# MoE1's second product with tokens on partitions, the domain weight applied where it leaves PSUM, and TensorE transposes to MoE2's input

## The chip, the cores and the metric

The kernel runs as one program on one core of a Trainium2 chip. The metric is device time in microseconds (us) of that core, from a launch with all inputs in HBM to the output in HBM. TensorE is called PE here, VectorE DVE, ScalarE ACT, GpSimd POOL and SyncE SP, as in the profile.

## The reference

Three steps follow one another on 2304 tokens (4 batches of 576) of 512 features.

```
# chunked attention: 8 heads of 64, chunks of 64 tokens
scores = (q_c @ k_c^T) / 8;  attn = softmax(scores);  x = attn @ v_c        # x: [2304, 512]
# MoE1: 4 experts, 512 -> 1024 -> 512
p = domain_probs / (domain_probs.sum(-1) + 1e-9)                            # [2304, 4], positive
x1 = sum over e of  p[:, e] * (max(x @ w1[e], 0) @ w2[e])
# MoE2: 512 -> 2048 -> 512
h = x1 @ w_in;  out = (h * clip(h + 3, 0, 6) / 6) @ w_out
```

All of it is fp32 to the caller, except that `w_in` and `w_out` arrive as 64-bit floats.

## The kernel before

**Blocks, sets, groups.** Tokens are cut into six blocks of 256 or 512 (`sizes`), and blocks are paired into three sets: 256 and 512, 512 and 256, 512 and 256. The hidden features of both MoEs are cut into groups of 512 columns: 8 groups for MoE1 (`G1`, two for each expert) and 4 for MoE2 (`G2`). In a set the order is group by group, and in a group first the one block, then the other. Only the first two groups of the first set run otherwise, in three parts of 256 tokens.

**Slots.** A group on a block is eight slots: four H slots (`h_slot`, first product, one per 128 hidden columns) and four Y slots (`y_slot`, second product). Each fp32 product is split: a tensor is kept as a high part that PE's fast fp32 format holds exactly and a low part, and three matmuls (high x high, high x low, low x high, the list `HL`) make one product. So an H slot is 12 matmuls of n columns, n the tokens of the block. In MoE1 a Y slot is also 12 matmuls of n columns: the weights are the stationary operand, the tokens move, and the result has features on partitions (four banks `psY`, one for each 128 features). In MoE2 the hidden activations are stationary, 512 weight columns move, and the result has tokens on partitions (n/128 banks), which is the layout of the output.

**What leaves PSUM.** PSUM has 2 banks for H, 4 for Y and 2 for attention. In MoE1 an H slot's bank is read by DVE alone (L434: u = max(psH, 0) * pb, where `pb` holds the domain weight of each token, broadcast over the partitions by a DMA from a scratch tensor in HBM). ACT then rounds u to the high part (L437), and one slot later DVE computes the low part u - high (L438). In MoE2 the bank is read by ACT (r = relu(psH + 3)) and one slot later by DVE (L447), followed by ACT's high part and DVE's low part (L451). After the fourth Y slot the Y banks are added into `acc` in SBUF (`finish`): by ACT's copy for the first group of a MoE, by DVE (L492) for the others. These additions are queued in `spread` and taken 2, 1, 1 and 0 at a time in the next four H slots. At MoE1's last group the sum is split again into MoE2's input x: high by ACT (L498), low by POOL (L499).

**What else runs.** Weights are loaded, rounded by ACT (L140) and subtracted by POOL (L141), 8 tiles for each group. In the first set's MoE1, from group 2 on, 32 tiles of MoE2's weights are turned from 64-bit to 32-bit floats (`Convert`): ACT takes absolute value and low word (L162, L163), DVE runs five operations (L167, L168, L171, L178, L182), POOL two (L183, L184). Two `cm` tiles limit how many are under way. Attention for the second and third set is computed in items of 512 columns, spread over the MoE slots of the set before.

**What sets the order.** All instructions are issued in an order that the program writes out. For each slot it issues: prepared loads (`pre`), the slot's matmuls, attention matmuls (`tail`), the low parts left from the slot before (`late`), attention's vector work (`early`), the slot's own reading of PSUM (`now`), some additions from `spread`, and the conversion steps (`post`). A planner, `fit`, puts attention and conversion steps into slots by an estimate of DVE's load in each slot (`busy`).

## Time and profile before

| | |
|---|---|
| time, median of 3 runs | 1328.59 us (1327.57 to 1329.6) |
| profiled execution | 1329.72 us, of which the span is 1327.9 us |
| PE busy | 1277.5 us (96%) |
| DVE busy | 696.8 us (52%) |
| ACT busy | 457.0 us (34%) |
| POOL busy | 504.3 us (38%) |
| mean granted clock of PE | 0.984 |

The span is the time from the first to the last instruction. The busy time of PE overlaps: matmuls are pipelined and their ends are modelled, so a busy PE is not a PE at its pace. Its pace is read from the distance between starts, which is what the chain of waits shows. "x <- y" names the tile written and the tiles read; L412 is line 412 of the kernel before. The shares above are averages over stretches with different limits, so the views below are taken by stretch.

### The profile page before, as it was taken

How to read it: one execution, taken by the hardware profiler on the slowest of the kernel's cores; microseconds unless marked ns; L12 is line 12 of the kernel's file. 1: busy time of each engine (PE TensorE's matmuls, PEld its weight loads, DVE VectorE, ACT ScalarE, POOL GpSimd, SP SyncE). 2: the span in 40 equal slices, each digit the busy share in tenths (PEclk: the TensorE clock that was granted, in tenths of full speed). 3: DMA queues.
4: the chain of work that ended last, by engine and by line, in shares of the span. 5: the costliest groups of instructions: out<-in, count | busy, mean ns of one | idle time of the engine just before them, and what ended most of it. 6: DMA issues, size and time to landing. Idle time of an engine off the chain costs nothing.

```text
span 1327.9 us, 20991 instructions
## 1 busy us (share of the span) xinstructions
PE 1277.5 (96%) x8134; PEld 1109.9 (84%) x8134; DVE 696.8 (52%) x1200; ACT 457.0 (34%) x914; POOL 504.3 (38%) x382
## 2 busy tenths in 40 slices
PE   8999889788999999999999999999999999999998
PEld 7998778676888888888888888888888888888887
DVE  5648999989555653233354544654233333333443
ACT  4343334333344432322222344343322222234432
POOL 3324766657542223333323262322333333344330
PEclk9999899889999999999999999999999999999999
DMA  7426555554333324222223233423222222222211
GB/s 191 127 75 188 174 172 166 170 146 136 92 91 105 87 72 123 70 69 69 71 81 94 62 89 103 112 65 104 83 72 68 72 68 72 68 64 64 64 32 48
DMA packets 172548, 128.86 MB, mean 97 GB/s; under 512 B 66720, under 2 KB 141984, under 8 KB 172448
## 3 DMA queue, kind: packets, MB, share of 16 engines
q1 hardware_dynamic: 172448, 127.52, 33.2%
q8 instruction: 64, 1.05, 0.3%
q14 instruction: 36, 0.29, 0.1%
HBM read 114.33 MB, written 13.14 MB: 96 GB/s over the span
## 4 chain that ended last, share of the span: by engine, by line
PE 80%; DVE 16%; ACT 2%; issue 1%; DMA 0%; SPq 0%; POOL 0%; ACTq 0%; DVEq 0%; POOLq 0%
PE psH L412 38%; PE psY L471 23%; PE psY L473 15%; DVE gt L438 3%; DVE cm L168 3%; DVE cm L171 2%; DVE cm L167 2%; DVE u L434 1%; DVE ce L178 1%; PE psS L306 1%; DVE acc L492 1%; DVE cm L182 1%; PE psP L338 1%; DVE e L330 1%; PE psX L349 1%
## 5 line engine op out<-in xcount | busy, mean ns | idle before, releaser
L412 PE MATMUL psH<-x,ws 128*128 128x256 f32 (+1 forms) x3552 | 634.9, 337 | 29.8 <-DVE u L434 27.5
L141 POOL TENSOR_TENSOR ws<-wr,ws 128x512 fp32r<-128x512 f32 x288 | 386.4, 1353 | 723.3 <-ACT ws L140 676.4
L412 PEld LDWEIGHTS psH<-x,ws 128*128 128x128 f32 x3552 | 550.5, 193 | 101.3 <-DVE u L434 31.1
L471 PE MATMUL psY<-gt,ws 128*128 128x256 f32 (+1 forms) x2400 | 413.2, 330 | 0.1
L471 PEld LDWEIGHTS psY<-gt,ws 128*128 128x128 f32 x2400 | 354.9, 188 | 49.4 <-DVE gt L438 0.5
L437 ACT CAST gt<-u 128x256 fp32r<-128x256 f32 (+1 forms) x200 | 100.1, 501 | 511.5 <-DVE u L434 510.8
L434 DVE SCALAR_TENSOR_TENSOR u<-psH,pb 128x256 f32<-128x256 f32 (+1 forms) x200 | 107.6, 538 | 313.4 <-PE psH L412 312.6
L473 PE MATMUL psY<-ws,gt 128*128 128x512 f32 x864 | 204.4, 393 | 0.0
L473 PEld LDWEIGHTS psY<-ws,gt 128*128 128x128 f32 x864 | 160.7, 188 | 34.3
L140 ACT CAST ws<-wr 128x512 fp32r<-128x512 f32 x288 | 171.1, 617 | 3.6 <-DMA wr<-in_moe_w_dram 2.9
L438 DVE TENSOR_TENSOR gt<-u,gt 128x256 fp32r<-128x256 f32 (+1 forms) x200 | 142.1, 711 | 56.2 <-ACT gt L437 54.5
L492 DVE TENSOR_TENSOR acc<-psY,acc 128x512 f32<-128x512 f32 (+1 forms) x226 | 125.4, 574 | 48.1 <-PE psY L473 36.1
L443 ACT ACTIVATE r<-psH,three 128x256 f32<-128x256 f32 (+1 forms) x96 | 55.7, 580 | 162.5 <-PE psH L412 161.2
L447 DVE SCALAR_TENSOR_TENSOR u<-r,psH 128x256 f32<-128x256 f32 (+1 forms) x96 | 53.0, 552 | 102.7 <-ACT r L443 101.9
L451 DVE SCALAR_TENSOR_TENSOR gt<-u,gt 128x256 fp32r<-128x256 f32 (+1 forms) x96 | 74.0, 771 | 41.5 <-ACT gt L450 41.4
L450 ACT ACTIVATE gt<-u 128x256 fp32r<-128x256 f32 (+1 forms) x96 | 50.6, 527 | 43.7 <-DVE u L447 43.5
L183 POOL TENSOR_TENSOR w<-w,ce 128x512 f32<-128x512 f32 x32 | 49.1, 1534 | 25.8 <-DVE ce L178 24.2
L184 POOL TENSOR_TENSOR ce<-w,cm 128x512 f32<-128x512 f32 x32 | 43.9, 1372 | 2.5
L499 POOL TENSOR_TENSOR x<-acc,x 128x256 fp32r<-128x256 f32 (+1 forms) x24 | 26.1, 1103 | 32.8 <-ACT x L498 32.8
L171 DVE SCALAR_TENSOR_TENSOR cm<-w,cm 128x512 uint32<-128x512 uint32 x32 | 35.8, 1118 | 1.1
L168 DVE TENSOR_SCALAR cm<-cm 128x512 uint32<-128x512 uint32 x32 | 33.4, 1045 | 1.1
L167 DVE TENSOR_SCALAR cm<-cm 128x512 f32<-128x512 f32 x32 | 29.3, 916 | 4.1 <-ACT cm L162 4.1
(45 smaller groups left out, 364.1 us busy)
## 6 DMA issues: line engine op xcount, KB each, us to landing
wr<-in_moe_w_dram SPq DMA_DIRECT2D x192, 256.0 KB, 2.8
wr<-win SPq DMA_DIRECT2D x48, 256.0 KB, 2.8
wr<-wout SPq DMA_DIRECT2D x48, 256.0 KB, 2.6
w<-in_moe_w_in_dram SPq DMA_DIRECT2D x16, 512.0 KB, 5.0
w<-in_moe_w_out_dram SPq DMA_DIRECT2D x16, 512.0 KB, 4.8
out_dram<-acc SPq DMA_DIRECT2D x18, 256.0 KB, 2.1
win<-ce SPq DMA_DIRECT2D x16, 256.0 KB, 3.5
wout<-ce SPq DMA_DIRECT2D x16, 256.0 KB, 3.0
```

The lines of the kernel that those rows point to most:

```text
L140: nc.scalar.copy(t[:, 0], self.t)
L141: (eng or nc.gpsimd).tensor_tensor(out=t[:, 1], in0=self.t, in1=raw(t[:, 0]), op=ALU.subtract)
L168: nc.vector.tensor_scalar(out=mu, in0=mu, scalar1=4, scalar2=1, op0=ALU.logical_shift_left, op1=ALU.logical_shift_right)
L171: nc.vector.scalar_tensor_tensor(out=mu, in0=self.t[:, :, 1], scalar=0x80000000, in1=mu, op0=ALU.bitwise_and, op1=ALU.bitwise_or)
L412: nc.tensor.matmul(ps[:, :n], w[:, a, d, :], xt[blk, d][:, b, cs], start=(d == 0 and i == 0), stop=(d == KD - 1 and i == len(HL) - 1),)
L434: nc.vector.scalar_tensor_tensor(out=u, in0=ps[:, :n], scalar=0.0, in1=pb[g // HS, blk][:, cs], op0=ALU.max, op1=ALU.mult)
L437: nc.scalar.copy(gt[:, 0], u)
L438: late.append(lambda: nc.vector.tensor_tensor(out=gt[:, 1], in0=u, in1=raw(gt[:, 0]), op=ALU.subtract))
L451: late.append(lambda: nc.vector.scalar_tensor_tensor(out=gt[:, 1], in0=u, scalar=1.0 / 6.0, in1=raw(gt[:, 0]), op0=ALU.mult, op1=ALU.subtr ...
L471: nc.tensor.matmul(ps[:, :n], w[:, a, j * P:(j + 1) * P], gt[:, b, :], start=first, stop=last)
L473: nc.tensor.matmul(ps, gt[:, a, j * P:(j + 1) * P], w[:, b, :], start=first, stop=last)
L492: nc.vector.tensor_tensor(out=acc[:, j, :], in0=ps[:, :m], in1=acc[:, j, :], op=ALU.add)
```

## The change

The second product of MoE1 takes the form that MoE2 has: hidden activations stationary, 512 weight columns moving, tokens on partitions. A domain weight is then one number per partition, so it no longer needs to be broadcast over partitions, and it is applied where the Y banks are added up instead of on the hidden activations. The weights `pn` are kept in SBUF, one column per token tile and expert. ACT reads an H bank first (relu, rounded to the high part), and DVE reads it a slot later for the low part, max(psH, 0) - high. The sum for MoE2 has tokens on partitions and MoE2's first product needs features there, so PE transposes it, four 128x128 tiles into one Y bank, from which ACT takes the high part and DVE the low part (`turn`).

The x tiles of a block become one tile, the four tiles of the conversion become one, the numbers taken from `spread` become 2, 2, 0, 0 (`TAKE`), and the planner's load estimate follows: one DVE operation for an H slot of MoE1 instead of two. Two paddings in SBUF (a wider row for `prs`, a tile `gap` of 16 columns that POOL sets to zero once) only move addresses.

```diff
@@ domain weights @@
-        nc.sync.dma_start(out=pT.rearrange("e (p r) -> p e r", p=P), in_=n)
+        nc.vector.tensor_tensor(out=pn, in0=pr, in1=s.unsqueeze(2).to_broadcast([P, R, NE]), op=ALU.mult)
-        nc.sync.dma_start(out=t, in_=pT[e:e + 1, t0:t0 + n].to_broadcast([P, n]))
...
+    TAKE = (2, 2, 0, 0)
+    def turn(src, dst):
+        ps = bank("y", "psT")
+        for d in range(KD):
+            nc.tensor.transpose(ps[:, d * P:(d + 1) * P], src[:, d * P:(d + 1) * P], ident)
+        p3 = ps.rearrange("p (d t) -> p d t", d=KD)
+        def low():
+            nc.vector.tensor_tensor(out=dst[:, :, 1, :], in0=p3, in1=raw(dst[:, :, 0, :]), op=ALU.subtract)
+        nc.scalar.copy(dst[:, :, 0, :], p3)
+        late.append(low)
@@ slot, after the low parts left from the slot before @@
+        while turns:
+            turn(*turns.popleft())
@@ h_slot, MoE1 @@
-                nc.vector.scalar_tensor_tensor(
-                    out=u, in0=ps[:, :n], scalar=0.0, in1=pb[g // HS, blk][:, cs], op0=ALU.max, op1=ALU.mult
-                )
-                nc.scalar.copy(gt[:, 0], u)
-                late.append(lambda: nc.vector.tensor_tensor(out=gt[:, 1], in0=u, in1=raw(gt[:, 0]), op=ALU.subtract))
+                nc.scalar.activation(gt[:, 0], ps[:, :n], AF.Relu)
+                late.append(lambda: nc.vector.scalar_tensor_tensor(
+                    out=gt[:, 1], in0=ps[:, :n], scalar=0.0, in1=raw(gt[:, 0]), op0=ALU.max, op1=ALU.subtract
+                ))
@@ y_slot @@
-            ys[:] = [bank("y", "psY")
-                     for _ in range(KD if g < G1 else n // P)]
+            ys[:] = [bank("y", "psY") for _ in range(n // P)]
-                    if g < G1:
-                        nc.tensor.matmul(ps[:, :n], w[:, a, j * P:(j + 1) * P], gt[:, b, :], start=first, stop=last)
-                    else:
-                        nc.tensor.matmul(ps, gt[:, a, j * P:(j + 1) * P], w[:, b, :], start=first, stop=last)
+                    nc.tensor.matmul(
+                        ps, gt[:, a, j * P:(j + 1) * P], w[:, b, :],
+                        start=f == 0 and i == 0, stop=f == GF - 1 and i == len(HL) - 1,
+                    )
@@ finish @@
+                if g < G1:
+                    p = pn[:, r, g // HS:g // HS + 1]
+                    if g == 0:
+                        nc.vector.tensor_scalar(out=t, in0=ps, scalar1=p, scalar2=None, op0=ALU.mult)
+                    else:
+                        nc.vector.scalar_tensor_tensor(out=t, in0=ps, scalar=p, in1=t, op0=ALU.mult, op1=ALU.add)
...
-                    nc.scalar.copy(t[:, 0], acc[:, j, :])
-                    nc.gpsimd.tensor_tensor(out=t[:, 1], in0=acc[:, j, :], in1=raw(t[:, 0]), op=ALU.subtract)
+                    turns.append((t, xt[blk][:, :, :, j * P:(j + 1) * P]))
@@ planner @@
-            busy[i] += vec(n)
-            busy[i + 1] += vec(n)
+            busy[i + 1] += vec(n) * (1 if gi % NG < G1 else 2)
...
```

On DVE, the four H slots of group 4 on block 0 (256 tokens) in the first set stood in this order before. `psY` here are the banks of group 3 on the 512-block, `cm` and `ce` belong to the conversion.

```order
L434 SCALAR_TENSOR_TENSOR u_2383<-psH_2381,pb_2274 128x256
L492 TENSOR_TENSOR acc_1026<-psY_2268,acc_1026 128x512
L492 TENSOR_TENSOR acc_1026<-psY_2269,acc_1026 128x512
L438 TENSOR_TENSOR gt_2382<-u_2383,gt_2382 128x256
L434 SCALAR_TENSOR_TENSOR u_2411<-psH_2409,pb_2274 128x256
L492 TENSOR_TENSOR acc_1026<-psY_2270,acc_1026 128x512
L438 TENSOR_TENSOR gt_2410<-u_2411,gt_2410 128x256
L434 SCALAR_TENSOR_TENSOR u_2430<-psH_2428,pb_2274 128x256
L492 TENSOR_TENSOR acc_1026<-psY_2271,acc_1026 128x512
L438 TENSOR_TENSOR gt_2429<-u_2430,gt_2429 128x256
L434 SCALAR_TENSOR_TENSOR u_2452<-psH_2450,pb_2274 128x256
```

They stand in this order after the change.

```order
L503 SCALAR_TENSOR_TENSOR acc_910<-psY_1994,pn_80,acc_910 128x512
L503 SCALAR_TENSOR_TENSOR acc_910<-psY_1995,pn_80,acc_910 128x512
L446 SCALAR_TENSOR_TENSOR gt_2092<-psH_2091,gt_2092 128x256
L503 SCALAR_TENSOR_TENSOR acc_910<-psY_1996,pn_80,acc_910 128x512
L503 SCALAR_TENSOR_TENSOR acc_910<-psY_1997,pn_80,acc_910 128x512
L446 SCALAR_TENSOR_TENSOR gt_2116<-psH_2115,gt_2116 128x256
L168 TENSOR_SCALAR cm_2133<-cm_2133 128x512
L169 TENSOR_SCALAR cm_2133<-cm_2133 128x512
L172 SCALAR_TENSOR_TENSOR cm_2133<-w64_913,cm_2133 128x512
L446 SCALAR_TENSOR_TENSOR gt_2137<-psH_2136,gt_2137 128x256
L179 TENSOR_SCALAR ce_2191<-cm_2133 128x512
L183 TENSOR_SCALAR cm_2133<-cm_2133 128x512
```

The operation that reads `u` from SBUF is gone from each slot; the low half of `gt` is the only operation of a slot and now reads the bank. All four additions stand ahead of the second low half, and the conversion's first three operations stand ahead of the third low half instead of behind the fourth read of the bank.

On PE, the end of the first set's MoE1 stood in this order before: group 7 on the 256-block and the 512-block, then MoE2's first group on both.

```order
L412 MATMUL psH<-x,ws 128x256 x48
L471 MATMUL psY<-gt,ws 128x256 x48
L412 MATMUL psH<-x,ws 128x512 x48
L471 MATMUL psY<-gt,ws 128x512 x48
L412 MATMUL psH<-x,ws 128x256 x48
L473 MATMUL psY<-ws,gt 128x512 x24
L412 MATMUL psH<-x,ws 128x512 x48
L473 MATMUL psY<-ws,gt 128x512 x12
```

The same place stands in this order after the change.

```order
L424 MATMUL psH<-x,ws 128x256 x48
L479 MATMUL psY<-ws,gt 128x512 x24
L424 MATMUL psH<-x,ws 128x512 x24
L378 MATMUL psT<-ident,acc 128x128 x8
L424 MATMUL psH<-x,ws 128x512 x24
L479 MATMUL psY<-ws,gt 128x512 x48
L424 MATMUL psH<-x,ws 128x256 x24
L378 MATMUL psT<-ident,acc 128x128 x8
L424 MATMUL psH<-x,ws 128x256 x12
L378 MATMUL psT<-ident,acc 128x128 x8
L424 MATMUL psH<-x,ws 128x256 x12
L479 MATMUL psY<-ws,gt 128x512 x24
```

Y has 24 matmuls of 512 columns for 256 tokens instead of 48 of 256. Transposes of `acc` (`psT`) stand inside the H slots that follow: eight, two token tiles, behind the second H slot of group 7 on the 512-block for the 256-block's sum, and two times eight inside MoE2's first H slots of the 256-block for the 512-block's sum.

## Rows read from the trace of the kernel before

**Rows 1.** The chain of waits, last set: start us, length us, what.
```profile
925.11 10.90 PE psH L412 x48
936.01 11.20 PE psY L471 x48
947.21 5.75 PE psH L412 x48
952.95 5.46 PE psY L471 x48
...
1202.41 10.99 PE psY L473 x48
...
1219.25 5.49 PE psY L473 x24
```

**Rows 2.** PE in order of time: start us, us, line, operation, count.
```profile
116.02 5.62 PE L412 MATMUL psH<-x,ws 128*128 128x512 f32 x24
...
341.74 8.56 PE L412 MATMUL psH<-x,ws 128*128 128x512 f32 x37
```

**Rows 3.** The chain of waits, first set: attention pieces on PE.
```profile
48.79 0.62 PE psX L349 x32
...
66.62 0.44 PE psP L338 x4
67.05 1.08 PE psS L306 x32
```

**Rows 4.** Busy us (count) of PE, PEld, DVE, ACT, POOL; clock, DMA.
```profile
116.00:342.00 226.00, 190.15 (x1100) 162.86 (x1099) 212.93 (x303) 80.16 (x152) 150.12 (x103) 0.91 0.51 158
```

**Rows 5.** Waits between 116 and 342 us: total us, times, longest us.
```profile
ACT cm L162 <- POOL ce L184: 27.5, 9, 5.0
PE psH L412 <- DVE u L434: 27.4, 9, 6.5
```

**Rows 6.** The chain of waits in the stretch's first part.
```profile
120.49 1.46 DVE cm L167
...
126.15 1.70 DVE gt L438
```

**Rows 7.** DVE's groups by shape, 116 to 342 us: busy us, mean ns, idle before.
```profile
L171 DVE SCALAR_TENSOR_TENSOR cm<-w,cm 128x512 uint32<-128x512 uint32 x31 | 35.1, 1132 | 1.1
L168 DVE TENSOR_SCALAR cm<-cm 128x512 uint32<-128x512 uint32 x31 | 33.0, 1065 | 1.1
L167 DVE TENSOR_SCALAR cm<-cm 128x512 f32<-128x512 f32 x31 | 28.9, 932 | 4.1 <-ACT cm L162 4.1
L438 DVE TENSOR_TENSOR gt<-u,gt 128x512 fp32r<-128x512 f32 x20 | 23.6, 1180 | 1.0 <-ACT gt L437 0.8
L438 DVE TENSOR_TENSOR gt<-u,gt 128x256 fp32r<-128x256 f32 x20 | 19.5, 973 | 0.0
...
L434 DVE SCALAR_TENSOR_TENSOR u<-psH,pb 128x512 f32<-128x512 f32 x20 | 13.7, 683 | 0.0
...
L492 DVE TENSOR_TENSOR acc<-psY,acc 128x512 f32<-128x512 f32 x20 | 13.2, 678 | 0.0
L434 DVE SCALAR_TENSOR_TENSOR u<-psH,pb 128x256 f32<-128x256 f32 x20 | 8.3, 416 | 2.8 <-PE psH L412 2.7
L492 DVE TENSOR_TENSOR acc<-psY,acc 128x256 f32<-128x256 f32 x20 | 7.9, 414 | 0.0
```

**Rows 8.** The same view of the last set, 925 to 1320 us.
```profile
L438 DVE TENSOR_TENSOR gt<-u,gt 128x512 fp32r<-128x512 f32 x32 | 22.2, 692 | 15.0 <-ACT gt L437 14.6
```

**Rows 9.** All engines in order of time: three conversion operations that wait for nothing.
```profile
245.29 0.42 DVE L167 TENSOR_SCALAR cm<-cm 128x512 f32<-128x512 f32 x1
...
245.74 0.43 DVE L168 TENSOR_SCALAR cm<-cm 128x512 uint32<-128x512 uint32 x1
...
246.20 0.69 DVE L171 SCALAR_TENSOR_TENSOR cm<-w,cm 128x512 uint32<-128x512 uint32 x1
```

**Rows 10.** PE's waits over the whole run.
```profile
PE psH L412 <- DVE u L447: 2.0, 3, 1.4
```

More of the change, by code (lines that the diff above doesn't have):

```diff
@@ L72, in fused_kernel @@
     NGI = NG * len(sets)
+    PRS = 48
     ident = const.tile([P, P], F32, name="ident")
@@ L357, in s5 @@
             for i, p in enumerate(self.ps):
-                if self.c0 == 0:
-                    full = sizes[self.blk]
-                    xt[self.blk, p] = xp.tile([P, 2, full], F32R, tag=f"x{full}", name="x", bufs=8)
-                t = xt[self.blk, p][:, :, self.c0:self.c0 + self.n]
+                if self.blk not in xt:
+                    new_x(self.blk)
+                t = xt[self.blk][:, p, :, self.c0:self.c0 + self.n]
                 w = self.nm * CH
@@ L372, in stages @@
                     (self.s4_pe, self.s4), (self.s5_pe, self.s5)]
-    late, spread = deque(), deque()
+    late, spread, turns = deque(), deque(), deque()
+    TAKE = (2, 2, 0, 0)
[8 more added lines that the diff above has]
+        late.append(low)
     def slot(pe, now, pre, tail, early, post, take):
@@ L453, in mid @@
                 ))
-        slot(pe, now, pre, tail, early, post, (2, 1, 1, 0)[f])
+        slot(pe, now, pre, tail, early, post, TAKE[f])
     def y_slot(gi, view, f, pre, tail, early, post):
@@ L479, in now @@
                 full = sizes[blk]
-                shape = [P, KD, full] if g < G1 else [P, full // P, DM]
-                accs[blk] = xp.tile(shape, F32, tag=f"acc{full}", name="acc", bufs=1)
-            acc = accs[blk][:, :, c0:c0 + n] if g < G1 else accs[blk]
-            m = n if g < G1 else DM
+                accs[blk] = xp.tile([P, full // P, DM], F32, tag=f"acc{full}", name="acc", bufs=1)
+            j0 = c0 // P
+            acc = accs[blk]
             if g == G1 - 1:
-                for j in range(KD):
-                    xt[blk, j] = xp.tile([P, 2, n], F32R, tag=f"x{n}", name="x", bufs=8)
+                new_x(blk)
             def finish(j, ps):
-                if g in (0, G1):
-                    nc.scalar.copy(acc[:, j, :], ps[:, :m])
+                t = acc[:, j0 + j, :]
+                r = starts[blk] // P + j0 + j
+                if g < G1:
[4 more added lines that the diff above has]
+                        nc.vector.scalar_tensor_tensor(out=t, in0=ps, scalar=p, in1=t, op0=ALU.mult, op1=ALU.add)
+                elif g == G1:
+                    nc.scalar.copy(t, ps)
                 else:
-                    nc.vector.tensor_tensor(out=acc[:, j, :], in0=ps[:, :m], in1=acc[:, j, :], op=ALU.add)
+                    nc.vector.tensor_tensor(out=t, in0=ps, in1=t, op=ALU.add)
                 if g == NG - 1:
-                    r0 = starts[blk] + j * P
-                    nc.sync.dma_start(out=out[r0:r0 + P, :], in_=acc[:, j, :])
+                    nc.sync.dma_start(out=out[r * P:(r + 1) * P, :], in_=t)
                 if g == G1 - 1:
-                    t = xt[blk, j]
-                    nc.scalar.copy(t[:, 0], acc[:, j, :])
-                    nc.gpsimd.tensor_tensor(out=t[:, 1], in0=acc[:, j, :], in1=raw(t[:, 0]), op=ALU.subtract)
+                    turns.append((t, xt[blk][:, :, :, j * P:(j + 1) * P]))
             spread.extend(lambda j=j, ps=ps: finish(j, ps) for j, ps in enumerate(ys))
@@ L527, in fused_kernel @@
         if kind == "h":
-            busy[i] += vec(n)
-            busy[i + 1] += vec(n)
+            busy[i + 1] += vec(n) * (1 if gi % NG < G1 else 2)
             if i > 0:
                 g_, (_, _, n_), _, _ = slots[i - f - 1]
-                count, w = (KD, n_) if g_ % NG < G1 else (n_ // P, DM)
-                busy[i] += vec(w) * min((2, 1, 1, 0)[f], max(count - (0, 2, 3, 4)[f], 0)) * ( g_ % NG not in (0, G1))
+                done = min(TAKE[f], max(n_ // P - sum(TAKE[:f]), 0))
+                busy[i] += vec(DM) * done * (g_ % NG != G1)
+                busy[i + 1] += vec(DM) * done * (g_ % NG == G1 - 1)
     def fit(i, work):
@@ L679, in fused_kernel @@
         at(pre, 3 * GF * 2, lambda: w64.extend(
-            xp.tile([P, 512, 2], U32, tag="x512", name="w64", bufs=8) for _ in range(4)
+            [big[:, i] for big in [xp.tile([P, 4, 512, 2], U32, tag="x512", name="w64", bufs=2)] for i in range(4)]
         ))
@@ L693, in fused_kernel @@
             ends.append(i2)
-        for si, st in enumerate(sets):
-            for e in range(NE):
-                if si or e:
-                    for blk in st:
-                        i = min(
-                            n for n, (gi, view, _, _) in enumerate(slots)
-                            if gi == si * NG + e * HS and view[0] == blk
-                        )
-                        at(pre, when(begins[i] - 10), lambda e=e, blk=blk: load_pb(e, blk))
         for si in range(1, len(sets)):
```

32 lines of the change are left out of this document (13 added, 19 removed).

## Prediction

> **What bounds the kernel now.** I read the table of stretches first, then PE's waits, then the chain of waits, then the groups by line with shapes kept apart.
>
> PE is busy for nearly the whole run, so the question is where its matmuls don't run at their own pace. Away from any wait the chain shows that pace [rows 1]: four H slots of 512 tokens 10.90 us, four Y slots 11.20 us, the same for 256 tokens 5.75 and 5.46 us. One group over a 512-block and a 256-block is thus 33.31 us. MoE2's Y, which already has tokens on partitions, takes 10.99 and 5.49 us.
>
> The stretch in which PE does not hold that pace runs from 116.02 us (H of group 2, block 1) to 341.74 us (H of group 7, block 1) [rows 2], and holds five such pairs plus two attention items. An item costs PE 0.44 us for four transposes, 1.08 for the scores and 0.62 for the product with V [rows 3], 2.14 us. So PE needs 5 x 33.31 + 2 x 2.14 = 170.8 us there and takes 225.7: 55 us too long. In that stretch DVE is busy 212.9 of 226 us, PE's granted clock falls to 0.91, and POOL is busy 150.1 us [rows 4]. PE's largest recorded wait there is for DVE's u (27.4 us) [rows 5]; matmuls at the lower clock add to it. The chain there lies on DVE [rows 6], in the `Convert` operations and gt: this stretch is DVE-bound, because the 32 conversions share it with the first set's MoE1. Elsewhere PE is its own bound, so each PE microsecond added there counts in full.
>
> Why DVE is full there is seen in the groups by shape [rows 7]. L434, which reads PSUM, takes 683 and 416 ns. L438, with both inputs in SBUF and the same sizes, takes 1180 and 973 ns; in the last set, with POOL quieter, its 512 form takes 692 ns [rows 8]. L167, L168 and L171 average 932, 1065 and 1132 ns, against 0.42, 0.43 and 0.69 us when nothing stands in their way [rows 9]. DVE operations in SBUF lose time beside POOL here, and those that read PSUM lose none.
>
> **The change, part by part.** The sum is made against the profiled execution's 1329.72 us (span 1327.9 and 1.8 around it), which is 1.1 above the median of 1328.59.
>
> *DVE in the stretch.* Before, an H slot cost DVE L434 and L438. Now ACT does relu straight from PSUM (the cast's place, so ACT's count stays) and DVE does one operation, (max(psH,0) - gt), reading PSUM and one SBUF tensor: L434's form. I price it as L434, so 43.1 us of L438 [rows 7] leave and the 22.0 us of L434 stay as the new low half. The trace shows no subtract of this form; the bounds are L434's 683 and L438's 1180 ns. L492 was 13.2 us for 20 of 512 columns and 7.9 for 20 of 256, 21.1; now there are 30 of 512 columns with a scalar per partition, 30/20 x 13.2 = 19.8 us. DVE's busy time becomes 212.9 - 43.1 - 1.3 = 168.5.
>
> *What comes late next.* The blocked time of L167, L168 and L171 is (28.9 + 33.0 + 35.1) - 31 x 1.54 = 49 us. POOL's 150 us of work now fall into a shorter stretch T, and I let the blocked time grow as POOL's share does. DVE's idle 13.1 us I keep. T = 168.5 + 13.1 + 49 x (226/T - 1) gives T = 191. PE's own need is 170, so DVE still ends last, and the stretch shrinks by 35 us. The bounds are 56 (PE becomes the bound) and 0 (POOL or the conversions' own chain of ACT, DVE and POOL already set the pace).
>
> *Y on PE.* Same number of columns: 12 matmuls of n columns before, 3n/128 of 512 now. Outside the stretch there are 17 Y groups of 512 tokens (22 in all, since block 1's first two groups run in halves, less five) at 10.99 - 11.20 = -0.21, and 23 of 256 (28 less five) at +0.03: -2.9 us. Inside, PE has room.
>
> *The transposes.* 18 token tiles x 4. Four fp32 transposes of 128x128 stand on the chain at 0.44 us [rows 3], so 18 x 0.44 = 7.9 us, all where PE is the bound. They sit behind the H matmuls of a later slot than the accumulation they read, so I expect no wait; the bound is one DVE operation (0.68) per pair, 6 us. By the Trainium skill ("TensorE: Matmul & The Clock Gate", Part 4, "PE-mode transpose") one transpose takes about 275 ns in a kernel: 72 would be 20 us, an estimate that speaks against the change; the sum below would end 12 us higher. The trace's four in 0.44 us decide here.
>
> *The H bank.* Before, a bank came free after one DVE operation; now after ACT's relu and then DVE's low half, which is issued a slot later. With two banks, slot f+2 waits for it. For 256 tokens that is one slot, 5.75/4 = 1.44 us. MoE2 already frees its bank by ACT and then DVE, and cost PE 2.0 us [rows 10] over 24 groups; the 40 MoE1 groups outside the stretch at that rate give 3.3 us (bounds 0, and 0.2 us at two slots of each of the 23 small groups, 9). Behind a late relu on ACT stand weight casts and the conversions' first step; behind a late low half on DVE stand the accumulations that free the Y banks.
>
> *At no cost.* The broadcast of the weights (one store, 24 loads) leaves SP's queue, where its landing ended no PE wait. POOL's x-low (24 operations) goes to DVE as 18 operations outside the stretch, where DVE is idle half of the time; were that cover gone, 18 x 0.7 = 12 us. MoE1's first accumulation moves from ACT to DVE, 18 x 0.7, mostly before the stretch.
>
> Sum: 1329.7 - 35 - 2.9 + 7.9 + 3.3 = 1303.0; on the median's scale **1302 us**.
>
> **Rivals.**
>
> *PE becomes the bound at once* (chance 0.12). If L438's going also frees POOL enough that the conversions run unblocked, the stretch falls to PE's 170: 56 instead of 35, so 1281. For it: PE's clock would stay up. Against: POOL's share would be 0.88, and conversions already lose most where POOL is dense.
>
> *The scalar operand counts as a second SBUF input* (0.08). The new accumulation reads PSUM, acc and pn. If pn makes it behave as L438 did, each of the 30 in the stretch costs 1180 - 692 = 0.49 us more, 14.6 us of DVE; solving again, T = 202 and the time 1313. The Trainium skill ("SBUF — State Buffer", section "Who interferes with whom") has a DVE operation with two SBUF inputs blocked by GpSimd, and one with a single SBUF input not; it could be read so, though another page ("DVE: scalar operands, raw-bit mode, write accounting and state across instructions", the paragraph on pointer scalars) says that such a scalar takes no second stream. No row of before shows one.
>
> *ACT's queue comes onto the path: slower* (0.08). In the stretch ACT stands 27.5 us in nine waits of the conversions' first step for POOL [rows 5], up to now harmless, since a late cast only delays gt. Now the relu stands behind it, DVE's low half behind the relu, and DVE has the conversions behind that. If all nine land on DVE and grow with POOL's share, 27.5 x 226/191 = 32.5, T is 223 and the time 1334. From 27 us on, 0.87 us per conversion, the gain no longer pays for PE's additions. Against: most of these steps stand behind the relu of slots whose bank is not wanted until four Y slots later.
>
> *The stretch is bound by the conversions, not by DVE's total* (0.04): no gain there, 8 us added, but part of the waits for e and u vanish: within 0.2% of before.
>
> **How the numbers follow.** The forecast has 0.68 with its own range 1288 to 1317 (T from 178 to 205). Of the rivals, 1281 lies just outside the low end and 1313 inside. The range 1284 to 1323 holds 8 in 10. About 0.2%, 2.7 us, is what a measurement of this kernel tells from no change. Faster: 0.68 + 0.12 + 0.08 and a little of the last, 0.88; same 0.04; slower 0.08.
>
> **What would show it.** Right: between the start of group 2's second block and group 7's second block about 191 us, PE's clock near 1, DVE still the fullest engine there; the low half at 0.68 and 0.42 us, also beside POOL; the accumulation at 0.68; four transposes in 0.44 us; PE waiting for DVE's low half by a few us outside the stretch. Wrong: the stretch at 215 or more with ACT's relu as what DVE waits for; accumulations near 1.1 us; Y at another pace than MoE2's; transposes that wait for acc.

## The result and the profile after

The changed kernel takes 1308.24 us (median of 4 runs, 1306.12 to 1310.69) against 1328.68 before: a ratio of 0.9847, 95% interval 0.9828 to 0.9866. That is faster by 1.5%, 6 us above the forecast of 1302 and inside its range. The profiled execution took 1307.79 us, span 1306.0.

PE in order of time gives the two ends of the stretch (columns as in [rows 2], which they answer; L424 is now H, L378 the transposes), and eight transposes.

```profile
118.66 5.60 PE L424 MATMUL psH<-x,ws 128*128 128x512 f32 x24
...
320.64 5.61 PE L424 MATMUL psH<-x,ws 128*128 128x512 f32 x24
326.09 1.03 PE L378 MATMUL psT<-ident,acc 128*128 128x128 f32 x8
```

The stretch runs from 118.66 to 320.64 us: 202.0 us instead of 225.7, so 23.7 saved where 35 were forecast. It begins 2.6 us later than before, and what follows it takes 985.4 us instead of 986.2. These three make up the whole: -23.7 + 2.6 - 0.8 = -21.9, and the spans differ by 1327.9 - 1306.0 = 21.9.

The stretch and the rest, as in [rows 4]: length, busy us and counts of PE, PEld, DVE, ACT, POOL, PE's granted clock, DMA share, GB/s.

```profile
118.66:320.64 201.98, 181.50 (x977) 151.45 (x976) 176.60 (x248) 77.15 (x150) 144.52 (x103) 0.95 0.56 172
320.64:1306.00 985.36, 978.78 (x5553) 833.46 (x5551) 365.51 (x622) 316.60 (x625) 290.86 (x222) 1.00 0.27 75
```

DVE's 176.6 us of work are close to what the forecast had: 168.5 + 49 x (226/191 - 1) = 177.5. But the stretch is 25.4 us longer than that work, where the forecast kept DVE's idle time of before, 13.1 us. PE, with 181.5 us, is now busier there than DVE.

The waits in the stretch, answering to [rows 5] (total us, times, longest us):

```profile
PE psH L424 <- DVE gt L446: 20.1, 11, 4.3
...
DVE gt L446 <- ACT gt L445: 12.2, 9, 2.2
ACT cm L163 <- POOL ce L185: 11.3, 4, 3.1
```

DVE's groups by shape there, answering to [rows 7] (busy us, mean ns | idle before):

```profile
L169 DVE TENSOR_SCALAR cm<-cm 128x512 uint32<-128x512 uint32 x30 | 33.7, 1122 | 1.0
L172 DVE SCALAR_TENSOR_TENSOR cm<-w,cm 128x512 uint32<-128x512 uint32 x30 | 33.6, 1119 | 1.0
L168 DVE TENSOR_SCALAR cm<-cm 128x512 f32<-128x512 f32 x30 | 27.8, 927 | 5.6 <-ACT cm L163 5.5
L503 DVE SCALAR_TENSOR_TENSOR acc<-psY,pn,acc 128x512 f32<-128x512 f32 x31 | 21.7, 742 | 3.1 <-PE psY L479 3.1
L179 DVE TENSOR_SCALAR ce<-cm 128x512 uint32<-128x512 uint32 x30 | 17.9, 595 | 0.9
L183 DVE TENSOR_SCALAR cm<-cm 128x512 uint32<-128x512 uint32 x30 | 13.8, 460 | 1.0
L446 DVE SCALAR_TENSOR_TENSOR gt<-psH,gt 128x512 fp32r<-128x512 f32 x20 | 13.5, 685 | 9.7 <-ACT gt L445 9.7
L446 DVE SCALAR_TENSOR_TENSOR gt<-psH,gt 128x256 fp32r<-128x256 f32 x20 | 8.3, 417 | 2.5 <-ACT gt L445 2.5
```

L446, the new low half, takes 685 and 417 ns beside POOL, like the L434 by which it was priced. The accumulation L503 takes 742 ns, not 678; it takes 748 behind the stretch too, where POOL is quieter, so it is not blocked. The conversion's three steps (L168, L169, L172) are blocked as much as before: 3.17 us together, against 3.13 in [rows 7] and 1.54 in [rows 9].

The chain of waits in the last set, answering to [rows 1]:

```profile
936.82 10.88 PE psH L424 x48
947.70 10.88 PE psY L479 x48
958.58 5.64 PE psH L424 x48
964.23 5.46 PE psY L479 x24
```

Y of 512 tokens at 10.88 is what MoE2's form was to give (10.99) and a little better, and H of 256 tokens fell from 5.75 to 5.64, which was not expected. One pair of blocks is 32.86 us, 0.45 less than the 33.31 of before. That accounts for what follows the stretch: 16 pairs (two sets of eight groups) and a last Y of 512 give -7.5, 18 tiles' transposes at 0.40 give +7.2, and PE's waits stay at about 2 us (2.2 before, 2.1 after), -0.4 together against the measured -0.8.

**Where PE's time in the stretch goes.** PE's own need is now 5 x 32.86 + 2 x 2.14 = 168.6 us; the stretch takes 33.4 more. Its recorded waits are 20.5 us (20.1 above, and 0.4 for attention), and a mean clock of 0.95 over 202 us costs about 10. Before, the stretch had 54.9 us too many: 27.4 of waits for u [rows 5], about 20 from the clock of 0.91, and one more wait, from the same view of before (psP waits for attention's e):

```profile
PE psP L338 <- DVE e L330: 8.3, 2, 4.2
```

So waits fell from 35.7 to 20.5 us and the clock's part from 20 to 10. What is left is not DVE running out of time, since DVE is idle 25 us. One H phase shows what it is. All engines in order of time, group 5 on the 512-block:

```profile
241.77 5.60 PE L424 MATMUL psH<-x,ws 128*128 128x512 f32 x24
...
243.15 1.40 DVE L503 SCALAR_TENSOR_TENSOR acc<-psY,pn,acc 128x512 f32<-128x512 f32 x2
244.47 0.42 DVE L168 TENSOR_SCALAR cm<-cm 128x512 f32<-128x512 f32 x1
244.49 1.57 POOL L185 TENSOR_TENSOR ce<-w,cm 128x512 f32<-128x512 f32 x1
244.75 0.60 ACT L445 ACTIVATE gt<-psH 128x512 fp32r<-128x512 f32 x1 [1.72 <-PE psH L424]
244.92 1.42 DVE L169 TENSOR_SCALAR cm<-cm 128x512 uint32<-128x512 uint32 x1
...
246.02 3.19 POOL L142 TENSOR_TENSOR ws<-wr,ws 128x512 fp32r<-128x512 f32 x2
246.38 1.68 DVE L172 SCALAR_TENSOR_TENSOR cm<-w,cm 128x512 uint32<-128x512 uint32 x1
247.47 0.60 ACT L445 ACTIVATE gt<-psH 128x512 fp32r<-128x512 f32 x1 [1.61 <-PE psH L424]
...
248.10 1.40 DVE L179 TENSOR_SCALAR ce<-cm 128x512 uint32<-128x512 uint32 x1
...
249.53 0.43 DVE L183 TENSOR_SCALAR cm<-cm 128x512 uint32<-128x512 uint32 x1
...
249.88 1.28 DVE L446 SCALAR_TENSOR_TENSOR gt<-psH,gt 128x512 fp32r<-128x512 f32 x2
...
250.61 8.42 PE L424 MATMUL psH<-x,ws 128*128 128x512 f32 x24 [3.24 <-DVE gt L446]
...
256.83 0.69 DVE L446 SCALAR_TENSOR_TENSOR gt<-psH,gt 128x512 fp32r<-128x512 f32 x1 [2.25 <-ACT gt L445]
```

PE finishes its first two H slots at 247.4, and ACT's two relus are done at 245.35 and 248.07. DVE's order has the conversion's five steps between the additions and the low halves; three of them are blocked (1.42, 1.68 and 1.40 us), so the two low halves come from 249.88 on. Of the POOL work beside them only the first piece (L185) belongs to a conversion; the second (L142) is the low part of two ordinary weight tiles, so weight loading blocks a conversion as well. PE has waited 3.24 us for its bank. Now DVE runs out of work, because PE has to compute the next slot first: DVE's 0.69 us at 256.83 follows 2.25 us of idle time. PE and DVE wait in turn, and after the wait PE's next slot runs at half the clock (same columns as the stretches above):

```profile
250.61:256.20 5.59, 5.59 (x13) 4.43 (x14) 3.84 (x6) 0.00 (x0) 1.97 (x2) 0.50 0.99 350
```

A granted clock of 0.50, 1.2 GHz of 2.4, turns two slots that take 5.6 us into 8.42. This one blocked conversion thus cost PE 3.2 us of waiting and 2.8 of clock.

The other waits are alike. Of the 40 low halves in the stretch, 22 come behind a whole conversion in DVE's order, at times with additions or attention's steps between. The eleven that PE waits for are all among these 22, and the conversions ahead of them took 5.1 us each in the mean, those ahead of the other eleven 3.7. DVE's waits for relu (12.2 us) come from PE's side in eight cases of nine: ACT had been idle until PE finished the slot.

### The profile page after: what moved, and what is told of

Read it like the earlier page. It is cut to its first block, busy times and chain, and to the rows that moved or that the text cites. A ratio compares the mean times of both kernels' runs of the same rounds, so it can differ in the third digit from the quotient of the medians.

```text
span 1306.0 us, 19473 instructions
## 1 busy us (share of the span) xinstructions
PE 1269.9 (97%) x7534; PEld 1082.4 (83%) x7534; DVE 601.6 (46%) x990; ACT 439.2 (34%) x880; POOL 474.7 (36%) x359
## 4 chain that ended last, share of the span: by engine, by line
PE 81%; DVE 13%; ACT 2%; DMA 1%; issue 1%; SPq 1%; POOL 1%; DVEq 0%; ACTq 0%; POOLq 0%
PE psH L424 39%; PE psY L479 38%; DVE cm L172 2%; DVE cm L169 2%; DVE cm L168 2%; PE psS L303 1%; DVE ce L179 1%; DVE acc L503 1%; DVE acc L507 1%; DVE gt L446 1%; DVE cm L183 1%; PE psX L346 1%; DVE e L327 1%; PE psT L378 1%; PE psP L335 1%
## 5 line engine op out<-in xcount | busy, mean ns | idle before, releaser
L142 POOL TENSOR_TENSOR ws<-wr,ws 128x512 fp32r<-128x512 f32 x288 | 384.1, 1346 | 758.0 <-ACT ws L141 732.2
L424 PE MATMUL psH<-x,ws 128*128 128x256 f32 (+1 forms) x3552 | 630.7, 335 | 24.6 <-DVE gt L446 23.0
L424 PEld LDWEIGHTS psH<-x,ws 128*128 128x128 f32 x3552 | 545.5, 191 | 99.1 <-DVE gt L446 27.9
L479 PE MATMUL psY<-ws,gt 128*128 128x512 f32 x2592 | 607.2, 391 | 0.0
L479 PEld LDWEIGHTS psY<-ws,gt 128*128 128x128 f32 x2592 | 482.0, 188 | 98.9
L445 ACT ACTIVATE gt<-psH 128x256 fp32r<-128x256 f32 (+1 forms) x200 | 95.8, 479 | 514.2 <-PE psH L424 514.0
L446 DVE SCALAR_TENSOR_TENSOR gt<-psH,gt 128x256 fp32r<-128x256 f32 (+1 forms) x200 | 107.5, 539 | 233.8 <-ACT gt L445 233.8
L503 DVE SCALAR_TENSOR_TENSOR acc<-psY,pn,acc 128x512 f32<-128x512 f32 x126 | 89.2, 746 | 168.1 <-PE psY L479 168.1
L507 DVE TENSOR_TENSOR acc<-psY,acc 128x512 f32<-128x512 f32 x54 | 36.0, 687 | 44.8 <-PE psY L479 44.8
L185 POOL TENSOR_TENSOR ce<-w,cm 128x512 f32<-128x512 f32 x32 | 43.6, 1362 | 2.5
L172 DVE SCALAR_TENSOR_TENSOR cm<-w,cm 128x512 uint32<-128x512 uint32 x32 | 35.9, 1123 | 1.1
L169 DVE TENSOR_SCALAR cm<-cm 128x512 uint32<-128x512 uint32 x32 | 35.5, 1110 | 1.1
L168 DVE TENSOR_SCALAR cm<-cm 128x512 f32<-128x512 f32 x32 | 30.1, 940 | 6.2 <-ACT cm L163 6.1
L319 ACT ACTIVATE e<-e 128x512 f32<-128x512 f32 x18 | 11.4, 633 | 52.9 <-DVE e L315 52.9
L363 DVE TENSOR_TENSOR x<-psX,x 128x128 fp32r<-128x128 f32 (+1 forms) x56 | 15.8, 324 | 26.7 <-ACT x L362 25.2
L163 ACT ACTIVATE cm<-w 128x512 f32<-128x512 f32 x32 | 21.5, 673 | 11.6 <-POOL ce L185 11.6
```

What stands on the lines that cost most here:

```text
L142: (eng or nc.gpsimd).tensor_tensor(out=t[:, 1], in0=self.t, in1=raw(t[:, 0]), op=ALU.subtract)
L168: nc.vector.tensor_scalar(out=m, in0=m, scalar1=W_LEAST, scalar2=W_MOST, op0=ALU.max, op1=ALU.min)
L169: nc.vector.tensor_scalar(out=mu, in0=mu, scalar1=4, scalar2=1, op0=ALU.logical_shift_left, op1=ALU.logical_shift_right)
L172: nc.vector.scalar_tensor_tensor(out=mu, in0=self.t[:, :, 1], scalar=0x80000000, in1=mu, op0=ALU.bitwise_and, op1=ALU.bitwise_or)
L424: nc.tensor.matmul(ps[:, :n], w[:, a, d, :], xt[blk][:, d, b, cs], start=(d == 0 and i == 0), stop=(d == KD - 1 and i == len(HL) - 1),)
L445: nc.scalar.activation(gt[:, 0], ps[:, :n], AF.Relu)
```

## The experiments

All have the same stretch, H of group 2 on block 1 to H of group 7 on block 1, whatever their total. "One look" is a single time; the others are medians of 4 runs, with the 95% interval of their ratio to the kernel before. The columns from the stretch on are read from one profiled execution of each kernel. "Waits" are PE's for DVE.

| kernel | time us | ratio, 95% | stretch us | conversions in it | DVE busy | waits | clock |
|---|---|---|---|---|---|---|---|
| before | 1328.7 | 1 | 225.7 | 31 | 212.9 | 35.7 | 0.91 |
| old evacuation | 1329.4, one look | | 217.4 | 30 | 200.3 | 32.1 | 0.94 |
| new evacuation alone | 1322.9, one look | | 216.5 | 31 | 188.1 | 28.0 | 0.91 |
| old estimate | 1312.7, one look | | 208.2 | 31 | 186.7 | 25.2 | 0.94 |
| order | 1314.4 | 0.9879 to 0.9915 | 209.1 | 31 | 179.4 | 27.9 | 0.93 |
| after | 1308.2 | 0.9828 to 0.9866 | 202.0 | 30 | 176.6 | 20.5 | 0.95 |
| late load | 1303.9 | 0.9802 to 0.9831 | 201.7 | 30 | 176.9 | 20.1 | 0.95 |
| late load, spread to 0 | 1295.9 | 0.9737 to 0.9766 | 183.7 | 27 | 158.3 | 7.8 | 0.98 |
| spread to 20 | 1296.3 | 0.9744 to 0.9777 | 178.2 | 24 | 148.5 | 5.8 | 1.00 |
| late load, spread to 20, order | 1301.3 | 0.9780 to 0.9812 | 183.8 | 25 | 151.4 | 9.1 | 0.98 |
| late load, spread to 20 | 1291.7 | 0.9706 to 0.9735 | 178.3 | 24 | 148.9 | 5.9 | 1.00 |
| late load, spread to 40 | 1296.1 | 0.9742 to 0.9774 | 173.7 | 22 | 132.7 | 2.2 | 1.00 |
| no POOL steps | 1284.0, one look | | 177.1 | 30 | 141.3 | 5.3 | 1.00 |
| no transposes | 1304.9, one look | | 200.3 | 30 | 176.6 | 20.7 | 0.96 |

### Which part of the change earned it

**The old evacuation in the changed kernel** (DVE writes u, as before; the domain weight stays at the accumulation):

```diff
-                nc.scalar.activation(gt[:, 0], ps[:, :n], AF.Relu)
-                late.append(lambda: nc.vector.scalar_tensor_tensor(
-                    out=gt[:, 1], in0=ps[:, :n], scalar=0.0, in1=raw(gt[:, 0]), op0=ALU.max, op1=ALU.subtract
-                ))
+                nc.vector.tensor_scalar(out=u, in0=ps[:, :n], scalar1=0.0, scalar2=None, op0=ALU.max)
+                nc.scalar.copy(gt[:, 0], u)
+                late.append(lambda: nc.vector.tensor_tensor(out=gt[:, 1], in0=u, in1=raw(gt[:, 0]), op=ALU.subtract))
```

> The changed kernel with MoE1's H banks read as before: DVE writes max(psH, 0) to SBUF, ACT rounds it, DVE subtracts in SBUF; the rest of the change (Y's layout, the weight at the accumulation, the transposes, the planner's estimate) stays. Theory: the gain of the stretch is the SBUF subtract that went, so the stretch comes back to 220 to 232 us and the time to 1325 to 1338, with the subtract at about 1.1 us for 512 tokens there and 0.69 elsewhere. Rival: the gain comes from the fewer accumulations or from where the planner puts the conversions; the stretch stays under 208 and the time under 1314.

```profile
124.83:342.21 217.38, 185.16 (x977) 153.26 (x976) 200.31 (x286) 78.31 (x150) 145.36 (x101) 0.94 0.51 159
```

The stretch goes back by 15.4 of the 23.7 us, a little less than expected, and 6 more are lost ahead of it (it begins at 124.83), which brings the time to 1329.4. The rival (under 208 us) did not come out.

**The new evacuation alone**, in the kernel before: the same lines exchanged the other way. The domain weight has no place in this version and is left out of the sum.

> The kernel before, with only the reading of MoE1's H banks changed (ACT's relu from the bank, DVE's low half from the bank); the domain weight is left out of the computation, its loads stay, and so do Y's layout and the planner's estimate. Theory: the stretch shrinks from 226 to 198 to 208 us by this part alone and the time to 1301 to 1311. Rival: without the planner's new estimate and Y's layout it gains less than 10 us and the time stays above 1318.

```profile
118.61:335.15 216.54, 188.49 (x1098) 162.64 (x1097) 188.10 (x264) 79.11 (x152) 144.38 (x103) 0.91 0.53 164
```

The rival came out: 9.2 us of the 23.7, though DVE's load fell by 24.8. DVE's idle time grew to 28 us, and the clock stayed at 0.91. The evacuation is worth 9 alone and 15 in the changed kernel, so the parts do not add.

**The planner's estimate of before** in the changed kernel:

```diff
-            busy[i + 1] += vec(n) * (1 if gi % NG < G1 else 2)
+            busy[i] += vec(n)
+            busy[i + 1] += vec(n)
```

> The changed kernel with the planner's load estimate of before (two DVE operations for each MoE1 H slot, one in the slot and one in the next), nothing else undone. The new evacuation alone left the stretch at 216.5 us, the whole change has 202.0. Theory A, the planner's new placement is the other part of the gain: stretch 210 to 217 and time 1316 to 1323. Theory B, the rest of the change (fewer and wider accumulations, x's low half off POOL, Y's form) is: stretch at most 205, time 1306 to 1311.

```profile
118.56:326.71 208.15, 182.94 (x977) 152.75 (x976) 186.68 (x252) 78.78 (x152) 146.11 (x102) 0.94 0.54 167
```

208.2 us falls between the two theories. In the changed kernel the new placement of the conversions is worth about 6 us. If the parts added, the other 8 of the step from 216.5 to 202.0 would belong to the remaining edits together (fewer and wider accumulations, x's low half off POOL, Y's form). I have not separated these further, and single looks and parts that don't add leave this open.

### What is left in the stretch

**No POOL steps**: an ACT copy in the place of the conversion's two POOL operations, with the low word of the 64-bit floats left out.

```diff
-            nc.gpsimd.tensor_tensor(out=self.low, in0=self.low, in1=self.e, op=ALU.mult)
-            nc.gpsimd.tensor_tensor(out=self.e, in0=self.low, in1=m, op=ALU.add)
+            nc.scalar.copy(self.e, m)
```

> The changed kernel without POOL's two operations of each conversion (the low word of the 64-bit floats is left out; ACT copies the high part), so that POOL's work in the stretch falls from 144 to about 60 us. Theory B (total): the conversions' DVE operations lose their blocked time, DVE's busy time in the stretch falls by 30 us or more and the stretch to PE's 171 to 178 us. Theory A (order): a conversion still stands ahead of the low halves, but is shorter (2.5 instead of some 5 us); PE's waits for the low half fall to about half, 8 to 12 us, and the stretch to 180 to 190.

```profile
119.98:297.05 177.07, 171.71 (x978) 144.61 (x976) 141.30 (x247) 94.56 (x182) 55.48 (x41) 1.00 0.63 197
```

DVE's groups by shape in that stretch:

```profile
L168 DVE TENSOR_SCALAR cm<-cm 128x512 f32<-128x512 f32 x30 | 23.3, 775 | 16.8 <-ACT cm L163 16.6
...
L172 DVE SCALAR_TENSOR_TENSOR cm<-w,cm 128x512 uint32<-128x512 uint32 x30 | 20.8, 692 | 1.0
...
L169 DVE TENSOR_SCALAR cm<-cm 128x512 uint32<-128x512 uint32 x30 | 15.1, 505 | 1.0
```

With POOL busy 55 us instead of 145, the same three steps take 1.97 us instead of 3.17, PE's waits fall to 5.3 us and its clock is full. Theory B came out: DVE's busy time fell by 35 us and the stretch is 177. The conversions keep their places in this version, so most of what the stretch still loses comes from the time that they are blocked beside POOL. But DVE's total falls with it, and this run alone can't tell the total from the order.

**Order**: the conversions' DVE steps kept out of the first two H slots of each group and block, to take them from between the relu and its low half.

```diff
-    def fit(i, work):
+    def fit(i, work, ok=lambda j: True):
...
-        near = range(i, min(i + 14, NS))
+        near = [j for j in range(i, min(i + 14, NS)) if ok(j)]
...
+            calm = lambda j: not (slots[j][2] == "h" and slots[j][3] < 2)
-            i1 = fit(max([when(t0 + gap * i), *ends[-1:]]), 1.6)
-            i2 = fit(i1, 0.8)
+            i1 = fit(max([when(t0 + gap * i), *ends[-1:]]), 1.6, calm)
+            i2 = fit(i1, 0.8, calm)
```

> The changed kernel, with the planner kept from putting a conversion's DVE steps into the first two H slots of a group, so that no conversion stands in DVE's queue ahead of the low halves that free the two H banks. Theory A (order): of the 202 us that the stretch from group 2's second block to group 7's second block still takes, the 31 above PE's own 171 are PE waiting for a bank whose low half stands behind a conversion. Then PE's waits for the low half in the stretch fall from 20 us to under 8, the stretch to 180 to 190 us, and the time to 1290 to 1297. Theory B (total): DVE's work, with what POOL blocks of it, fills the stretch whatever its order; the stretch stays within 3 us of 202 and the time at 1305 to 1311.

```profile
PE psH L424 <- DVE gt L446: 24.4, 7, 4.4
```

It is slower than the changed kernel by 6 us, and neither theory came out: the stretch is 209.1. The conversions now stand in the slots that are left, and their backlog runs over into the H slots that were to be kept clear: ahead of six of the seven low halves that PE waits for, DVE has run a conversion from the Y slots and then two additions. There are fewer waits (7 instead of 11), each longer (3.5 us in the mean instead of 1.8).

**Spread to 20**: the 32 conversions are started over a longer time, until 20 us past the start of MoE2's first group instead of 25 us ahead of it.

```diff
-        gap = (begins[first[G1, "h", 0]] - 25 - t0) / len(pieces_)
+        gap = (begins[first[G1, "h", 0]] + 20 - t0) / len(pieces_)
```

> The changed kernel with the 32 conversions spread until 20 us after the start of MoE2's first group, by the planner's own estimate of time, where they ended 25 us ahead of it. Theory A, PE and DVE lose time to one another only where a conversion blocked by POOL stands between a relu and its low half, so what counts is how many stand in an H slot and how close: the stretch falls below 195 us, little is lost behind it (at most 6 us), time 1290 to 1300. Rival: the same conversions cost the same wherever they stand, the stretch falls to 185 to 190 but as much is lost behind it, time within 3 us of 1308; or MoE2's first weights come late and PE waits for ws behind 341 us, time over 1311.

The stretch and the rest (columns as before), then two waits of the stretch:

```profile
118.70:296.92 178.22, 172.36 (x978) 144.39 (x976) 148.50 (x217) 71.10 (x140) 124.27 (x89) 1.00 0.57 178
296.92:1291.60 994.68, 981.94 (x5553) 834.52 (x5551) 389.19 (x652) 321.73 (x635) 309.58 (x236) 1.00 0.27 77
```

```profile
DVE gt L446 <- ACT gt L445: 17.6, 14, 2.5
...
PE psH L424 <- DVE gt L446: 4.5, 5, 1.5
```

24 conversions remain in the stretch instead of 30, one in 7.4 us instead of one in 6.7, and PE's waits for the low half fall from 20.1 to 4.5 us. Theory A came out for the stretch and the time. The stretch becomes 23.8 us shorter and the rest 9.3 longer, more than the 6 allowed for. DVE's total in the stretch falls too, by 28 us, so this run doesn't separate how close the conversions stand from how many there are. DVE's idle time is now 29.7 us of 178: DVE waits for relu, and PE is the bound. The planner counts 1.6 + 0.8 = 2.4 us of DVE for a conversion; in the changed kernel its five steps take 0.93 + 1.12 + 1.12 + 0.60 + 0.46 = 4.2 us [the groups by shape above]. Its own limit on DVE's backlog therefore doesn't see the blocked ones.

**Late load, spread to 0, to 20 and to 40, and with the order kept clear** (the late load is below).

> The changed kernel with both the late load of the domain weights and the conversions spread to 20 us past the start of MoE2's first group. Apart they took 4 and 12 us off 1308. If the two act in different places, as their traces say (the start, and 119 to 370 us), they add: 1291 to 1293. If the spread also took up the time that the early load cost, 1295 to 1296.

> As the first, with the conversions spread to the start of MoE2's first group alone. Behind the stretch the wide spread lost 9.3 us, 5.4 of them in waits for u in MoE2's H slots, where conversions stood. If those come back and the stretch keeps a part of its gain (180 to 186 us), 1288 to 1291. If it is spacing that counts and the stretch goes back towards 190, 1293 to 1297.

> Late load and conversions spread to 40 us past the start of MoE2's first group. Ends at -25, 0 and 20 us gave 1303.9, 1295.9 and 1291.7, with 30, 27 and 24 conversions in the stretch and 4.2 us or more between PE's least there and what it took. If each conversion that leaves the stretch still pays: two or three fewer in it, 1288 to 1290. If the stretch is near PE's own 171 plus the one wait that is left, and MoE2's H slots take the loss, 1291 to 1295; if a MoE2 weight comes late, over 1296.

> As the last, and DVE's conversion steps are kept out of the first two H slots of each group and block, which alone cost 6 us. Theory A: that version failed because conversions piled up in the Y slots and ran over; with the wider spacing they fit, so PE's waits for the low half in the stretch and for u behind it (4.5 and 6.3 us with the spread alone) mostly go: 1286 to 1291. Rival: the place within a group matters little and the slots left are fuller, so it costs again: 1294 to 1298.

Late load and spread to 20 add up, as the first branch had it, and give the shortest time of a complete kernel, 1291.7 us. Ending at 0 leaves 6.8 us of waits for the low half in the stretch, one of them 3.2 us, and the time falls in the second branch. Ending at 40 brings the stretch to 173.7 but moves the loss behind it, into MoE2's H slots; the time, 1296.1, is just past what was expected of that, and PE waits for no weight there:

```profile
PE psH L424 <- DVE u L458: 12.5, 6, 5.8
```

Keeping H slots clear costs again, 1301.3, more than either branch allowed: the backlog comes out in one place behind the stretch, where DVE's transposes for attention stand behind it and PE's scores wait for them.

```profile
PE psS L303 <- DVE kT L289: 8.9, 1, 8.9
```

### The two costs outside the stretch

**No transposes on PE**; ACT and DVE read the sum in SBUF:

```diff
-        ps = bank("y", "psT")
-        for d in range(KD):
-            nc.tensor.transpose(ps[:, d * P:(d + 1) * P], src[:, d * P:(d + 1) * P], ident)
-        p3 = ps.rearrange("p (d t) -> p d t", d=KD)
+        p3 = src.rearrange("p (d t) -> p d t", d=KD)
```

> The changed kernel without its 72 transposes on PE: ACT and DVE read the sum in SBUF in the same place of the order, so MoE2's input is not transposed (that part is left out). If the transposes cost what their starts show, 18 times about 0.40 us, and hide behind nothing, the time falls from 1308.2 by 7 us to about 1301. If they also delay what follows them (the H matmuls wait for the turned x), by 10 or more. If PE would have waited there anyway, by under 3.

PE's waits behind the stretch, changed kernel first, then this one (gt L446 and gt L443 are the same operation), and this one's line of what is behind its stretch, columns as above:

```profile
PE psH L424 <- DVE u L458: 0.9, 3, 0.3
PE psH L424 <- DVE gt L446: 0.8, 1, 0.8
```

```profile
PE psH L421 <- DVE gt L443: 4.9, 3, 2.0
PE psH L421 <- DVE u L455: 2.4, 4, 1.5
```

```profile
317.96:1303.20 985.24, 972.98 (x5481) 827.02 (x5479) 367.36 (x622) 316.41 (x625) 291.32 (x222) 1.00 0.26 75
```

It takes 3 us less, in one look, and none of this comes from where the transposes stand. All 72 stand behind the stretch, and there the two executions take the same time: 985.36 us with them, 985.24 without. The difference lies ahead of that point, in code that both share: this execution begins its stretch 1.0 us earlier and passes it 1.6 us faster. Behind the stretch PE is busy 5.8 us less and waits 5.6 us more, so PE waits where the transposes stood. DVE's step from `acc` takes 840 ns here instead of 686, 2.8 us over 18, so up to half of the new wait is the experiment's own.

**Late load** of the domain weights, behind q, k and v in SP's queue:

```diff
         a.load_q()
-        domain_weights_load()
...
         b.load_v()
+        domain_weights_load()
```

(and their normalisation behind the first half of MoE1's first H products).

> The changed kernel with the load of the domain weights behind the loads of q, k and v in SP's queue, and their normalisation after the first half of MoE1's first H products. The stretch began 2.6 us later than before, after a wait of the first k transposes for their load. If the early load caused this, the stretch begins at about 116.0 to 116.5 and the time is 1305.5 to 1306.2, ratio to the changed kernel's 1308.2 about 0.998. If not, it begins at 118.5 and the time stays at 1308.

The first transposes of k and the first H products, changed kernel, then this one:

```profile
6.26 1.48 PE L282 MATMUL psT<-ident,kr 128*128 128x128 f32 x4 [0.70 <-DMA kr<-in_k_dram]
...
20.14 1.05 PE L424 MATMUL psH<-x,ws 128*128 128x256 f32 x6
```

```profile
5.36 1.06 PE L282 MATMUL psT<-ident,kr 128*128 128x128 f32 x4
...
18.33 1.63 PE L424 MATMUL psH<-x,ws 128*128 128x256 f32 x6
```

The load stands ahead of k and now puts one column per token tile into SBUF (`(p r) e -> p r e` became `(r p) e -> p r e`), so that the 18 tokens of a partition no longer lie side by side in HBM. Over the whole run there are 1264 more packets of under 512 B, although a store and 24 loads are gone. From 3.3 to 4.8 us the DMA engines of the changed kernel move 31 GB/s, where they move 191 before and 239 with the late load. The wait of 0.70 us for k goes and H's first products start 1.8 us earlier.

Neither branch came out as stated: the stretch begins later than the first allowed (117.87) and the time falls further, to 1303.9. The medians differ by 4.4 us, the profiled stretches' starts only by 0.8: a lower clock took back a part in this execution (six matmuls in 1.63 instead of 1.05 us). The start varies from one execution to the next, so all profiled ones are worth comparing. H's first products start at 17.50 and 18.31 us in the two with the old load, at 19.10 to 21.64 in the seven with the new one at its early place, and at 16.69 to 18.36 in the five with the late load. The one at 16.69 (late load, spread to 20, order) kept the full clock from 10 to 20 us, where the other four had 0.86 to 0.88, and its stretch begins at 115.35. The edit also moves the normalisation of the weights; what that alone gives is not separated.

## Why the prediction was right, and where not

The mechanism was right in kind: an operation that reads only SBUF left DVE's queue in the stretch, and undoing that alone takes 15.4 of the 23.7 us back. The total was closer than its terms. Forecast were -26.7 us, measured between the profiled executions -21.9. The stretch fell short by 11.3 and the start cost 2.6 that no term had; against this PE's own pace gave 4.6 more than forecast, 3.4 of waits outside the stretch did not come, and the transposes cost 0.7 less. That these partly cancel is luck; 0.4 us stays unaccounted for.

- **Y's pace** (-2.9 us forecast): too small, -7.5 behind the stretch with H's pace. Y of 512 tokens gave 0.32 us each where 0.21 was forecast, and H's 0.11 was not foreseen. This hid a part of the miss in the stretch.
- **DVE's work in the stretch**: 176.6 against 177.5 us, in part by luck. The blocked time of the three steps was to grow by 9 us with POOL's share; it stayed at 27.8 + 33.7 + 33.6 - 30 x 1.54 = 49 us, while the additions took 21.7 instead of 19.8 us. Operations that overlap are counted in full in the groups and once in the busy time, and this overlap fell from about 13 to 7 us. The reading that only operations with all their tensors in SBUF lose time beside POOL held.
- **"DVE's idle 13.1 us I keep"**: the step that failed. It took DVE to be the full engine, whose total sets the stretch. DVE's idle time doubled to 25.4 us, and the stretch saved 23.7 instead of 35. It is 17 to 41 us in the other versions, so DVE's total doesn't give the stretch: 179.4 us of DVE work took 209.1 us (order), 176.6 took 202.0, and 158.3 took 183.7 (late load, spread to 0). What the trace shows in its place is PE and DVE waiting in turn: each of PE's eleven waits for the low half follows a conversion in DVE's queue, most often one slowed beside POOL, and a lower clock after a wait adds to it. Without POOL's steps, or with the conversions spread by a tenth, the waits fall from 20.5 to 5.3 and 5.8 us. That it is a conversion's place ahead of the low half that counts, and not how much DVE work comes at once, is argued and not shown: the runs that removed the loss lowered DVE's total too, and the two that changed the place (order) were slower.
- **H bank** (+3.3 outside the stretch): 2.9 us of waits for gt, 2.1 of them ahead of the stretch and 0.8 behind it; MoE2's waits for u fell from 2.0 [rows 10] to 0.9, which was not foreseen.
- **Transposes** (+7.9): four take 0.40 us, 7.2 in all. Without them the time behind the stretch is the same to 0.1 us, with up to 2.8 us of the experiment's own in it. Where the transposes stand PE would have waited for DVE, so the terms for transposes and bank cover one another, which a sum over separate terms can't show.
- **"At no cost", the load of the weights**: wrong, by 2.6 us in the profiled executions (H's first products start at 20.14 instead of 17.50 us), and by 4.4 between the medians with the early and the late load. I looked at the broadcast that left SP's queue and not at the load that stayed ahead of k, whose layout the change alters. MoE1's first accumulation was to move to DVE mostly before the stretch; only 6 of its 18 tiles lie there, the other 12 in the later sets.
- **PE becomes the bound at once** (1281): not so, but the version with spread conversions comes to 178 us there, near PE's 169.
- **The scalar as a second SBUF input** (1313): refuted. L503 takes 742 ns in the stretch, with POOL busy 72% of it, and 748 behind it. The Trainium skill ("SBUF — State Buffer", "Who interferes with whom") lets a DVE instruction with at most one SBUF input, outside its two-port modes, run free of GpSimd. By the Trainium skill ("DVE: scalar operands, raw-bit mode, write accounting and state across instructions", "Pointer scalars") a scalar like `pn` does not take up the second stream. The trace agrees with both, but the scalar has a price of some 60 ns: 742 against 678 to 685 ns for the operations on 512 columns of a bank without it, and 745 to 748 ns where the bank and the scalar are the only inputs (L501).
- **ACT's queue** (1334): refuted. ACT's wait for POOL fell from 27.5 to 11.3 us; DVE's wait for relu, 12.2 us, comes nearly all from PE, which had to compute the slot first.

## What to carry to other kernels

When two engines hand buffers to one another, the busy total of the fuller one bounds the time from below only: look for what stands in its order between a producer and the release of the bank, and price a blocked operation there with the clock that the wait costs as well. Keeping that work out of chosen slots made this kernel slower twice. Work that only has to be done by some later point should be spread at the price that the trace shows for it, not at its undisturbed price. A small load whose layout changes belongs in the sum if it stands in a queue ahead of the first input.

## What the runs showed of the hardware that was not expected

- After a wait of 3.24 us PE's granted clock was 0.50 for the next 5.6 us, which cost 2.8 us, nearly as much as the wait itself.
- Four fp32 128x128 transposes inside a run of matmuls cost PE 0.40 us (326.09 to 326.88 for eight).
- A scalar per partition makes a DVE operation on 128x512 some 60 ns longer (742 to 748 against 678 to 687 ns), beside a busy POOL and a quiet one.
- One load of 36 KB in 16-byte pieces: from 3.3 to 4.8 us the DMA engines moved 31 GB/s instead of 191, and PE then waited 0.70 us for the first k tile behind it.
- H of 256 tokens went from 5.75 to 5.64 us with the same matmuls. Only the x tiles and the addresses changed; the cause stays open.
